# The first group of an adaLN transformer block: two projection tiles ahead of the rest, first attention slots loaded ahead of other stores, TensorE run on transposes before its work

## The chip, the core and the metric

One core of one Trainium2 chip runs the whole program. The metric is device microseconds of one execution; the median of three runs counts. Engines: PE is TensorE (matmuls and transposes, results in PSUM), DVE is VectorE, ACT is ScalarE, POOL is GpSimd, SP is SyncE, whose queue issues nearly all DMAs here. Each engine works through its own instructions in the order in which they were written; engines wait for each other by semaphores.

## The reference, cut to what matters

```python
x = A_x                                   # 1 x 2048 x 448, f32
mod = (silu(c) @ w_mod).reshape(1, 6, 1, -1)
sa, ca, ga, sb, cb, gb = (mod[:, 0], ..., mod[:, 5])
h = layernorm(x) * (1 + ca) + sa
# A: 16 heads of 28, causal window of 256
qkv = h @ wqkv
p = softmax(where(mask, q @ k.T * 28 ** -0.5, -1e9))
x = x + ga * ((p @ v) @ wo)
h = layernorm(x) * (1 + cb) + sb
x = x + gb * (mish(h @ w1 + b1) @ w2)     # 448 -> 1792 -> 448
```

## The kernel before

All products are kept near f32 precision by splitting each operand into a rounded part (names with `h` or hi) and the rest (`l`, lo) and adding three products. A 448-deep contraction is therefore 11 matmuls (`passes`, L183), taken over four chunks `ci` of 128 rows; the last chunk holds hi and lo of its 64 rows stacked.

The 2048 tokens are four groups `g` of 512 (`GT`). For each group the program normalises x (`gen_ln1`), transposes it (`tr`, four chunks of four 128x128 transposes) and applies the scale and shift columns `cols`, which gives `hh` and `hl` (`hT_hi` on ACT, `hT_y` and `hT_lo` on DVE). It then projects: tiles 0 to 6 are 128 rows of the q and k features each (q is features 0 to 447, k is 448 to 895, so tile 3 holds the end of q and the beginning of k), tiles v0 to v3 are V of 128 tokens each. `qk_out` (L308) takes a q/k tile out of PSUM (hi by ACT, lo by DVE) and stores it to the DRAM scratch `scr`: two DMAs for a tile of q rows or of k rows alone, four for tile 3, which has both.

Attention goes by slots: slot i is head i % 16 of group i // 16. `L(i)` (L562) loads q and k of a slot from `scr`. `A(i, t)` (L571) is a pass for the row maxima: a matmul `sA` on PE, then a max over it (`junk`, `mx`) on DVE. `M2` (L584) turns the maxima of two slots into rows (`mt` on PE, `mr` on DVE) and two small DMAs put them below q (`q<-mr`). `B(u)` (L600) is the score matmul proper (`sB`), exp on ACT (`P`, `Ph`), `SP` the rest `Pl` on POOL, `PV` the product with V. There are three units u per slot; the main loop (L920) runs B, SP, PV of its unit, the A of three slots ahead (`LEAD`), and between them takes steps of a filler, `fill_main(g)`, at `RATE[g]` credit per unit (about one microsecond of matmuls is one credit). The filler of group 0 holds what is left of group 0's projections, then the transposes and projections of group 1. `fill_side` carries the layernorm `ln1` of the next group and weight preparation, one step per unit from u = 2 on. At u = 48 the rest of group 0's fillers is drained; from there on before and after have the same instructions in the same order.

Ahead of the loop, in order: loads of c (`cT`), x of group 0, the first 896 columns of w_mod in four pieces `wm01`, then wqkv (`wqs`) in three parts of columns (`QCOLS`). DVE sums c-weighted pieces of w_mod into `acc01` (`mod_sum`, L143), PE turns that into columns (`mc`, L152), DVE copies them to `cols`. Splits of wqkv are shared by ACT (hi) and DVE and POOL (lo, `wql`). Three tiles, 0, 3 and 4, are worked through together (L397 to L401), stored, then `load_slot` loads slots 0 to 3, v0 to v3 and the tiles 1 and 5 run, and the A of slots 0 to 2 go with tiles 5, 2 and 6. `need` keeps running the filler until the tiles that a slot reads have been written.

Of the kernel before, what the change touches and what calls it, by code (L numbers as in the profile page):

```python
# [8 lines left out]
F32 = mybir.dt.float32  # L9
# [10 lines left out]
NEG = -1.0e30  # L20
# [31 lines left out]
def adaln_block(ctx: ExitStack, tc: tile.TileContext, x, wqkv, wo, w1, b1, w2, c, w_mod, out):  # L52
# [19 lines left out]
    vp, vp_s = pool("vp")  # L72
    st0, st0_s = pool("st0")
# [3 lines left out]

    ACT.add_instruction(mybir.InstLoadActFuncSet(
# [54 lines left out]
    cols = cst.tile([128, 4, 4], F32, name="cols")  # L133

# [3 lines left out]
    DVE.tensor_scalar(sT, sT, 1.0, None, op0=ALU.add)  # L138
    DVE.reciprocal(sT, sT)
    DVE.tensor_tensor(sT, sT, cT, op=ALU.mult)  # L140
# [100 lines left out]
    def hT_lo(p, ci, hh, hl, si):  # L241
        hT_y(p, ci, si)
        DVE.tensor_tensor(hl[:, ci], p, hh[:, ci].bitcast(F32), op=ALU.subtract)
# [58 lines left out]
    later = []  # L302

# [4 lines left out]
    def qk_out(g, m, p, st=None):  # L308
        st = st or qk.tile([128, 2, GT], F32R, name=f"st{g}_{m}", tag="qs", bufs=3)
# [11 lines left out]

        def put():
            for a, b, pa, ph in ((0, qn, 0, 2), (qn, 128, 1, 0)):
                if a < b:
                    dma(scr[r0 + a:r0 + b, pa:pa + 2, gs], st[a:b].bitcast(F32))
                    dma(scr[r0 + a:r0 + b, ph, gs], st[a:b, 0].bitcast(F32))
            done.add((g, m))

        return hi, lo, store

# [17 lines left out]
    def gen_qkv(g, tiles):  # L348
        first = {"v2": ("sB", 2), "v3": ("sB", 2), 1: ("pv", 1), 5: ("tr", 1)} if g == 0 else {}
        for m in tiles:  # L350
            p = bank(*first.get(m, ("mm", 2)), f"qk{g}_{m}")
# [17 lines left out]
    for k in range(4):  # L369
        mod_sum(k, wm01[k], acc01)  # L370
    pm = bank("sA", 2, "mc01")
# [8 lines left out]
    for ci in range(4):  # L380
        hi = wq3[:, ci, c0:c1]
        split_hi(wqs[ci][:, c0:c1], hi, ACT)
        split_lo(wqs[ci][:, c0:c1], hi, wql[:, min(ci, 2), c0:c1], ci, POOL)
    for i in range(2):
# [6 lines left out]
    for c0, c1 in QCOLS[1:]:  # L391
        for ci in range(4):
            split_hi(wqs[ci][:, c0:c1], wq3[:, ci, c0:c1], ACT)
    for (c0, c1), eng in zip(QCOLS[1:], (DVE, POOL)):
        for ci in range(4):
            split_lo(wqs[ci][:, c0:c1], wq3[:, ci, c0:c1], wql[:, min(ci, 2), c0:c1], ci, eng)
    first = [(m, bank(tag, b, f"qk0_{m}"), qk_passes(0, m)) for m, tag, b in ((0, "pv", 1), (3, "tr", 1), (4, "sA", 2))]  # L397
    for lo_n, hi_n in ((0, 3), (3, 6), (6, 11)):
        for m, p, ps in first:
            for n in range(lo_n, hi_n):  # L400
                PE.matmul(p, ps[n][1], ps[n][0], start=(n == 0), stop=(n == 10))  # L401
    for m, p, ps in first:
        st = st0.tile([128, 2, GT], F32R, name="st0_4") if m == 4 else None
        for f in qk_out(0, m, p, st):
            f()
        flush()
    st0_s.close()
    att, att_s = pool("att")

    identr = att.tile([128, 128], BF16, name="identr")  # L410
    mask = att.tile([128, 384], F32, name="mask")
# [656 lines left out]
```

## Time and profile before

| | |
|---|---|
| median of 3 runs | 740.03 us (738.38, 740.03, 742.38) |
| profiled execution | 743.38 us |
| its span, first to last instruction | 741.6 us |
| PE busy | 695.8 us, 94% |
| DVE, ACT, POOL busy | 378.9, 392.8, 331.4 us |
| moved by DMA | 83.86 MB |

How to read it: the page gives busy time by engine and the chain of work that ended last; the timeline lists instructions with their start, their length, and, in brackets, how long the engine had idled and what ended that; `x31` merges 31 like instructions that follow each other. PE's instructions overlap, so the price of one in a row of them is the distance between starts and not its length. [...] A matmul row is up to 0.4 us long though one can start each 0.23 us.

### The profile page before, as it was taken

The page shows a single profiled execution, that of the slowest core. Times are in us where ns is not written, and L with a number is a line of the kernel's source. Part 1 is how long each engine was busy: PE and PEld are TensorE (multiplying, and loading weights), DVE is VectorE, ACT ScalarE, POOL GpSimd, SP SyncE. Part 2 cuts the span into 40 slices and gives each one's busy share as a digit, 9 for nine tenths or more (in the row PEclk, how much of TensorE's full clock was granted, in tenths as well). Part 3 has the DMA queues.
Part 4 walks back from the last instruction along what each step waited for, and adds up shares of the span by engine and source line. Part 5 has one row for each costly group of instructions (what it writes and reads, how often), then busy time and mean ns, then how long its engine had stood idle before and what let it go on. Part 6 is the DMA issues. An engine that isn't in the chain of part 4 may idle for free.

```text
span 741.6 us, 11907 instructions
## 1 busy us (share of the span) xinstructions
PE 695.8 (94%) x3969; PEld 591.2 (80%) x3969; DVE 378.9 (51%) x1009; ACT 392.8 (53%) x740; POOL 331.4 (45%) x358
## 2 busy tenths in 40 slices
PE   3988989999999999999999889999999999999996
PEld 2866768778789888888887768878888888888885
DVE  4768546596765587665567843342323232413113
ACT  4416767676766677667778883343223222322221
POOL 4714788586666586666778854522010000000000
PEclk9898989999999999999999999999999999999999
DMA  8766644355274364453476155500200020001001
GB/s 211 204 226 221 166 139 129 94 178 179 86 226 154 100 221 144 133 179 92 145 215 204 50 187 164 145 24 1 100 0 1 1 99 1 1 0 50 1 0 50
DMA packets 48121, 83.86 MB, mean 113 GB/s; under 512 B 6126, under 2 KB 26108, under 8 KB 48060
## 3 DMA queue, kind: packets, MB, share of 16 engines
q1 hardware_dynamic: 48060, 83.10, 37.0%
q8 instruction: 32, 0.52, 0.3%
q14 instruction: 29, 0.24, 0.1%
HBM read 53.45 MB, written 29.36 MB: 112 GB/s over the span
## 4 chain that ended last, share of the span: by engine, by line
PE 77%; DVE 9%; DMA 7%; issue 3%; ACT 2%; POOL 1%; SPq 1%; DVEq 0%; POOLq 0%; ACTq 0%
PE z L813 19%; PE pv L639 9%; PE qk L294 6%; PE acc L990 6%; PE acc L991 6%; PE acc L989 6%; PE qk_v L294 5%; PE sA L578 4%; PE wo L294 4%; PE sB L608 4%; DMA k<-scr 3%; PE sB L619 3%; DVE junk L580 3%; PE et L650 1%; PE qk L401 1%
## 5 line engine op out<-in xcount | busy, mean ns | idle before, releaser
L629 POOL TENSOR_TENSOR Pl<-P,Ph 128x512 fp32r<-128x512 f32 (+2 forms) x192 | 236.7, 1240 | 94.0 <-ACT Ph L623 53.4
L580 DVE CUSTOM_DVE_ANT_0 junk<-sA,mask 128x384 f32<-128x384 f32 (+2 forms) x256 | 134.9, 527 | 116.7 <-PE sA L578 112.7
L622 ACT ACTIVATE P<-sB 128x512 f32<-128x512 f32 (+2 forms) x192 | 109.9, 572 | 65.0 <-PE sB L619 62.7
L821 DVE TENSOR_TENSOR al<-t,ah 128x512 fp32r<-128x512 f32 x56 | 38.8, 692 | 204.9 <-ACT ah L820 204.9
L819 ACT ACTIVATE t<-z,b1c 128x512 f32<-128x512 f32 x56 | 38.6, 689 | 193.3 <-PE z L813 182.4
L578 PE MATMUL sA<-k,q 84*128 84x384 f32 (+2 forms) x256 | 102.3, 403 | 10.7 <-DVE mx L580 6.0
L623 ACT ACTIVATE Ph<-sB 128x512 fp32r<-128x512 f32 (+2 forms) x192 | 109.3, 569 | 0.0
L813 PE MATMUL z<-hhf,w 128*128 128x512 f32 x224 | 89.4, 399 | 0.0
L813 PE MATMUL z<-hlf,w 128*128 128x512 f32 x224 | 88.7, 396 | 0.0
L989 PE MATMUL acc<-w2h,ah 128*128 128x448 f32 x224 | 82.2, 367 | 0.0
L990 PE MATMUL acc<-w2l,ah 128*128 128x448 f32 x224 | 82.0, 366 | 0.0
L991 PE MATMUL acc<-w2h,al 128*128 128x448 f32 x224 | 81.9, 366 | 0.0
L639 PE MATMUL pv<-Ph,v 128*60 128x256 f32 (+2 forms) x352 | 77.6, 294 | 3.0 <-ACT o L644 2.5
L639 PE MATMUL pv<-Pl,v 128*60 128x256 f32 (+2 forms) x352 | 74.5, 286 | 2.2 <-POOL Pl L629 2.1
L608 PE MATMUL sB<-q,k 86*128 86x256 f32 (+1 forms) x352 | 75.2, 288 | 1.0 <-DMA q<-mr 1.0
L813 PE MATMUL z<-hhf,w1l 128*128 128x512 f32 x168 | 66.4, 395 | 0.0
L608 PEld LDWEIGHTS sB<-q,k 86*128 86x128 f32 x352 | 62.6, 192 | 2.6 <-issue 1.0
L578 PEld LDWEIGHTS sA<-k,q 84*128 84x128 f32 x256 | 50.3, 197 | 16.8 <-DVE mx L580 10.1
L619 PE MATMUL sB<-fdmask,identr 128*128 128x128 bf16 (+1 forms) x320 | 60.9, 256 | 0.0
L639 PEld LDWEIGHTS pv<-Ph,v 128*60 128x60 f32 x352 | 45.5, 134 | 19.0 <-ACT o L644 6.0
L639 PEld LDWEIGHTS pv<-Pl,v 128*60 128x60 f32 x352 | 45.5, 133 | 11.8 <-POOL Pl L629 4.8
L644 ACT ACTIVATE o<-pv 60x512 f32<-60x512 f32 x64 | 37.8, 591 | 30.3 <-PE pv L639 29.8
(148 smaller groups left out, 1257.5 us busy)
## 6 DMA issues: line engine op xcount, KB each, us to landing
scr<-st SPq DMA_DIRECT2D x24, 512.0 KB
k<-scr SPq DMA_DIRECT2D x48, 252.0 KB
q<-scr SPq DMA_DIRECT2D x64, 168.0 KB
scr<-st SPq DMA_DIRECT2D x32, 256.0 KB
x<-x1d SPq DMA_DIRECT2D x10, 448.0 KB
xin<-in_A_x_dram SPq DMA_DIRECT2D x8, 448.0 KB
xr<-in_A_x_dram SPq DMA_DIRECT2D x16, 224.0 KB
x1d<-xr SPq DMA_DIRECT2D x16, 224.0 KB
```

The costliest lines, as they stand in the source:

```text
L294: PE.matmul(p, b, a, start=(n == 0), stop=(n == 10))
L578: PE.matmul(p[:, c0:384], q[0:84, t * 128:(t + 1) * 128], k[0:84, t * 128 + c0:t * 128 + 384], start=True, stop=True)
L580: DVE.tensor_tensor_reduce(out=junk[:, c0:384], in0=p[:, c0:384], in1=mask[:, c0:384], scale=1.0, scalar=-3.0e38, op0=ALU.add, op1=ALU.max ...
L608: PE.matmul(p[:, c:c + 128 * (t1 - t0)], k[:, jj * 128:(jj + 1) * 128], q[:, t0 * 128:t1 * 128], start=(n == 0), stop=False, skip_group_ch ...
L622: ACT.activation(P[:, c0:], p[:, c0:], AF.Exp, scale=SCALE)
L623: ACT.activation(Ph[u][:, c0:], p[:, c0:], AF.Exp, scale=SCALE)
L629: POOL.tensor_tensor(Pl[u][:, c0:], Pt[u][:, c0:], Ph[u][:, c0:].bitcast(F32), op=ALU.subtract)
L639: PE.matmul(pv[0:60, t0 * 128:t1 * 128], V[j % NV][:, h, :], P[u][:, c:c + 128 * (t1 - t0)], start=(P is Ph and b == 0 and n == 0), stop=F ...
L813: PE.matmul(zb[n], ps[m][1], ps[m][0], start=(m == 0), stop=(m == 10))
L989: PE.matmul(p, ah[n][:, ts], w2h[f], start=(f == 0), stop=False)
L990: PE.matmul(p, ah[n][:, ts], w2l[f], start=False, stop=False)
L991: PE.matmul(p, al[n][:, ts], w2h[f], start=False, stop=(f == NF - 1))
```

## The change

Only group 0 changes, up to unit 48:

- The load of c is issued from ACT's queue, ahead of everything; the fourth piece of w_mod is loaded and summed in two halves of 448 columns. The three small DVE steps on c come after the statistics of x.
- 64 transposes of the identity (`warm`) are added on PE: 50 ahead of the transposes of x, 2 after each of the first three token tiles, 8 behind `mc`.
- Constants (mask, the -1 rows of five k buffers, `fdf`) are made earlier on POOL, in a new pool `kq`.
- Two of the four `hT_y` steps go from DVE to ACT; splits of wqkv are spread in another order.
- Tiles 0 and 3 alone are worked through first. The k half of tile 3 and tile 0 are stored, then slots 0 and 1 are loaded, then come the other half of tile 3, tile 4, slots 2 and 3, and only then x of group 1.
- v0, v1 and tile 1 precede the first maxima; after that every A is followed by a filler step of up to four matmuls. Tile 6, the statistics of group 1's layernorm and all its transposes now stand in the main loop; side steps of group 0 start at u = 0; `RATE[0]` is 0.53.

```diff
+    cT = cst.tile([112, 4], F32, name="cT")
+    nc.scalar.dma_start(cT, c.rearrange("o (k p) -> p (o k)", p=112))
...
-    cT = cst.tile([112, 4], F32, name="cT")
-    dma(cT, c.rearrange("o (k p) -> p (o k)", p=112))
     x_load(0)
     wm01 = []
     for k in range(4):
         t = st0.tile([112, 2 * D], F32, name=f"wm01_{k}")
-        dma(t, w_mod[k * 112:(k + 1) * 112, 0:2 * D])
+        for s in (slice(0, 2 * D),) if k < 3 else (slice(0, D), slice(D, 2 * D)):
+            dma(t[:, s], w_mod[k * 112:(k + 1) * 112, s])
...
+        parts = [lambda: rows(qn, 128, 1, 0), lambda: rows(0, qn, 0, 2)]
+
         def put():
-            for a, b, pa, ph in ((0, qn, 0, 2), (qn, 128, 1, 0)):
...
+            while parts:
+                parts.pop(0)()
             done.add((g, m))
...
+    wb = bank("tr", 1, "warm")
+    def warm(n):
+        for _ in range(n):
+            PE.transpose(wb[:, 0:128], ident, ident)
+    warm(50)
...
+        if t < 3:
+            warm(2)
     for i in range(2):
         mod_cols(acc01[:, i * D:(i + 1) * D], pm[:, 4 * i:4 * i + 4])
+    warm(8)
...
     for ci in range(4):
         hT_hi(trs[ci], ci, hh, 0)
-        hT_lo(trs[ci], ci, hh, hl, 0)
-    x_load(1)
...
+        if ci % 2:
+            first_split(2 + ci // 2)
+            ACT.activation(trs[ci], trs[ci], AF.Identity, scale=cols[:, 1, ci:ci + 1], bias=cols[:, 0, ci:ci + 1])
+        hT_lo(trs[ci], ci, hh, hl, 0, ci % 2 == 0)
...
+    first_tiles([(0, bank("pv", 1, "qk0_0")), (3, bank("tr", 1, "qk0_3"))])
+    for m in (0, 3):
+        PARTS[0, m].pop(0)()
+    PARTS[0, 0].pop(0)()
+    L(0)
+    L(1)
+    flush()
+    split_cols(*QCOLS[1], (None, None, POOL, POOL))
+    first_tiles([(4, bank("sA", 2, "qk0_4"))])
+    flush()
...
-            yield from gen_qkv(0, VT + (1, 5, 2, 6))
+            yield from gen_qkv(0, VT[:2] + (1,) + VT[2:] + (5, 2, 6))
...
-    RATE = {0: 0.48, 1: 0.88, 2: 0.88, 3: 0.62}
+    RATE = {0: 0.53, 1: 0.88, 2: 0.88, 3: 0.62}
...
-    for i in range(LEAD + 1):
+    for i in range(2, LEAD + 1):
         load_slot(i)
-    need({f"v{t}" for t in range(4)}, 0)
-    load_slot(LEAD + 1)
+    x_load(1)
+    for _ in range(9):
+        fill0()
...
     for i in range(LEAD):
         for t in range(4):
             A(i, t)
-            if t % 2:
-                pipe.step()
-                next(fillers[0])
-                flush()
-            side_step(0)
+            fill0()
         if i % 2:
-            pipe.step()
-            next(fillers[0])
             M2(i // 2)
+            load_slot(LEAD + 1)
...
-            if v > 1:
+            if v > 1 or g == 0:
                 side_step(g)
```

On SP's queue, the first stores to `scr` (tiles as `st_` and the tile's number) and the first loads of q and k, before:

```order
L59 DMA scr<-st_0_291 128x2x512
L59 DMA scr<-st_0_291 128x512
L59 DMA scr<-st_3_296 64x2x512
L59 DMA scr<-st_3_296 64x512
...
L59 DMA scr<-st_4_303 128x2x512
L59 DMA scr<-st_4_303 128x512
L59 DMA q_0_350<-scr 84x512
L59 DMA k_0_353<-scr 84x512
```

and after:

```order
L59 DMA scr<-st_3_384 64x2x512
L59 DMA scr<-st_3_384 64x512
L59 DMA scr<-st_0_381 128x2x512
L59 DMA scr<-st_0_381 128x512
L59 DMA q_0_352<-scr 84x512
L59 DMA k_0_136<-scr 84x512
...
L59 DMA k_1_138<-scr 84x512
...
L59 DMA scr<-st_4_413 128x2x512
```

Eight stores stood ahead of the first load, now four do.

On PE, where the first transposes of group 1 (`tr`) stand, before, in the unit of the first score matmul:

```order
L294 MATMUL qk_6_541<-hl_223,wq_96 128x512
L578 MATMUL sA_2_577<-k_2_357,q_1_351 128x384
L578 MATMUL sA_3_581<-k_2_357,q_1_351 128x384
L232 MATMUL tr_587<-ident,xin_236 128x128 x4
L608 MATMUL sB_597<-q_0_350,k_0_353 128x384
```

and after, in unit 4:

```order
L661 MATMUL sB_708<-q_0_352,k_1_138 128x256
L672 LDWEIGHTS identr
L672 MATMUL sB_708<-fdmask,identr 128x128
L631 MATMUL sA_1_717<-k_4_144,q_2_433 128x256
L309 MATMUL qk_6_625<-hl_307,wq_100 128x512
L246 MATMUL tr_738<-ident,xin_456 128x128 x4
```

Tile 6 and the transposes have moved behind the first score matmuls, the transposes right behind the last matmul of tile 6.

On DVE, the end of group 1's statistics and the four normalising steps (`xin<-xin,mva,rsa`), which these transposes read, before:

```order
L193 BN_AGGR mva_483<-sta_513 128x2
L580 ISA junk,mx_479<-sA_0_519,mask 128x128
...
L222 TENSOR_SCALAR xin_236<-xin_236,mva_483,rsa_516 128x448
L580 ISA junk,mx_479<-sA_2_532,mask 128x384
...
L580 ISA junk,mx_479<-sA_3_537,mask 128x384
...
L317 TENSOR_TENSOR st_2_528<-qk_2_491,st_2_528 128x512
L588 CAST mr_555<-mt_553 8x128
```

and after:

```order
L207 BN_AGGR mva_630<-sta_700 128x2
L633 ISA junk,mx_687<-sA_1_717,mask 128x256
L633 ISA mx_687 128x1
L236 TENSOR_SCALAR xin_456<-xin_456,mva_630,rsa_703 128x448
L333 TENSOR_TENSOR st_6_725<-qk_6_625,st_6_725 128x512
L236 TENSOR_SCALAR xin_456<-xin_456,mva_630,rsa_703 128x448 x3
```

The normalising steps were spread between maxima; now one stands ahead of the lo step of tile 6 and three behind it, in one run.

## Rows read from the trace of the kernel before

**Rows 1.** The page: span of the profiled execution.
```profile
span 741.6 us, 11907 instructions
```
**Rows 2.** Windows of three stages: busy us of each engine, granted clock, DMA.
```profile
18.10:56.40 38.30, 34.49 (x139) 26.65 (x139) 27.91 (x63) 13.24 (x23) 17.29 (x45) 0.91 0.70 214
56.40:73.30 16.90, 14.74 (x83) 12.01 (x84) 13.62 (x35) 11.03 (x24) 8.09 (x8) 0.80 0.68 219
73.30:140.00 66.70, 60.54 (x388) 48.65 (x387) 37.31 (x143) 47.75 (x111) 51.31 (x54) 0.95 0.50 139
```
**Rows 3.** Chain that ended last, in order of time: start, us, what.
```profile
38.52 5.12 PE qk L294 x22
```
**Rows 4.** Windows of 1 us: granted clock is the third number from the end.
```profile
17.00:18.00 1.00, 0.00 (x0) 0.00 (x0) 0.40 (x4) 1.00 (x3) 0.92 (x2) 1.00 1.03 373
18.00:19.00 1.00, 0.87 (x2) 0.50 (x2) 0.85 (x2) 1.00 (x3) 0.43 (x1) 0.51 0.88 247
25.00:26.00 1.00, 1.00 (x6) 0.82 (x5) 1.00 (x2) 0.54 (x1) 1.00 (x2) 1.00 0.98 364
```
**Rows 5.** Timeline of SP, the first issues.
```profile
0.73 0.39 SPq L59 DMA_DIRECT2D cT<-in_c_dram  x1
1.18 0.98 SPq L59 DMA_DIRECT2D xin<-in_A_x_dram  x2
```
**Rows 6.** Timeline of DVE: last sum of w_mod, first scale step, last hl, lo steps.
```profile
13.40 1.15 DVE L147 SCALAR_TENSOR_TENSOR acc<-wm,sT,acc 112x896 f32<-112x896 f32 x1 [0.31 <-DMA wm<-in_w_mod_dram]
18.11 0.82 DVE L236 TENSOR_SCALAR tr<-tr,cols 128x512 f32<-128x512 f32 x1 [0.69 <-ACT hh L239]
23.32 0.69 DVE L243 TENSOR_TENSOR hl<-tr,hh 128x512 fp32r<-128x512 f32 x1
29.56 1.89 DVE L317 TENSOR_TENSOR st<-qk,st 128x512 fp32r<-128x512 f32 x3
```
**Rows 7.** Timeline of ACT: the four hh steps.
```profile
17.30 2.79 ACT L239 ACTIVATE hh<-tr,cols 128x512 fp32r<-128x512 f32 x4
```
**Rows 8.** Timeline of SP: first stores, first loads, a store and the load behind it.
```profile
30.27 6.91 SPq L59 DMA_DIRECT2D scr<-st  x8
37.29 1.19 SPq L59 DMA_DIRECT2D q<-scr  x1
...
42.59 0.90 SPq L59 DMA_DIRECT2D scr<-st  x2
48.75 0.32 SPq L59 DMA_DIRECT2D q<-scr  x1
```
**Rows 9.** Timeline of PE: first maxima, first mt, first score matmul, that of unit 48.
```profile
43.48 0.40 PE L578 MATMUL sA<-k,q 84*128 84x128 f32 x2
...
52.38 0.27 PE L586 MATMUL mt<-ident,mx 128*8 128x128 f32 x1 [0.38 <-DMA scr<-st]
...
56.37 0.41 PE L608 MATMUL sB<-q,k 86*128 86x384 f32 x1 [0.61 <-DMA q<-mr]
...
139.85 0.47 PE L608 MATMUL sB<-q,k 86*128 86x384 f32 x2
```
**Rows 10.** Timeline of POOL: the power step of group 1's layernorm.
```profile
49.35 1.05 POOL L207 TENSOR_TENSOR rsa<-rsa,mhalf 128x4 f32<-128x4 f32 x1
```
**Rows 11.** Timeline of DVE: the first normalising step of group 1.
```profile
50.44 0.51 DVE L222 TENSOR_SCALAR xin<-xin,mva,rsa 128x448 f32<-128x448 f32 x1 [0.80 <-POOL rsa L207]
```
**Rows 12.** PE's waits from 56.4 to 140 us: total, times, longest.
```profile
PE sA L578 <- DMA k<-scr: 3.7, 2, 2.8
PE tr L232 <- DVE hl L243: 2.2, 2, 1.1
```
**Rows 13.** Timeline of SP ahead of the longest of them.
```profile
89.54 3.01 SPq L59 DMA_DIRECT2D scr<-st  x4
...
93.48 0.51 SPq L59 DMA_DIRECT2D k<-scr  x1
```
**Rows 14.** Timeline of PE behind that load.
```profile
97.54 0.44 PE L578 MATMUL sA<-k,q 84*128 84x128 f32 x1 [2.85 <-DMA k<-scr]
```

More of the change, by code (lines that the diff above doesn't have):

```diff
@@ L133, in adaln_block, with k3_tile @@
     cols = cst.tile([128, 4, 4], F32, name="cols")
+    K3 = []
+    def k3_tile(pl, i):
+        t = pl.tile([86, GT + W], F32R, name=f"k3_{i}")
+        POOL.memset(t[64:86, :].bitcast(F32), -1.0)
+        K3.append(t)
+    for i in range(NK - 1):
+        k3_tile(kq, i)
+    mask = kq.tile([128, 384], F32, name="mask")
+    POOL.memset(mask, 0.0)
+    POOL.affine_select(mask, mask, pattern=[[1, 384]], compare_op=ALU.is_ge, fill=NEG, base=-1,
+                       channel_multiplier=-1)
+    POOL.affine_select(mask, mask, pattern=[[-1, 384]], compare_op=ALU.is_ge, fill=NEG, base=W,
+                       channel_multiplier=1)
     sT = cst.tile([112, 4], F32, name="sT")
     ACT.activation(sT, cT, AF.Exp, scale=-1.0)
-    DVE.tensor_scalar(sT, sT, 1.0, None, op0=ALU.add)
-    DVE.reciprocal(sT, sT)
-    DVE.tensor_tensor(sT, sT, cT, op=ALU.mult)
     def mod_sum(k, w, acc):
@@ L302, in adaln_block @@
     later = []
+    PARTS = {}
     def flush():
@@ L348, in gen_qkv @@
     def gen_qkv(g, tiles):
-        first = {"v2": ("sB", 2), "v3": ("sB", 2), 1: ("pv", 1), 5: ("tr", 1)} if g == 0 else {}
         for m in tiles:
-            p = bank(*first.get(m, ("mm", 2)), f"qk{g}_{m}")
+            p = bank("mm", 2, f"qk{g}_{m}")
             if isinstance(m, str):
@@ L368, in adaln_block @@
         next(ln0)
-    for k in range(4):
+    DVE.tensor_scalar(sT, sT, 1.0, None, op0=ALU.add)
+    DVE.reciprocal(sT, sT)
+    DVE.tensor_tensor(sT, sT, cT, op=ALU.mult)
+    for k in range(3):
         mod_sum(k, wm01[k], acc01)
+    for s in (slice(0, D), slice(D, 2 * D)):
+        mod_sum(3, wm01[3][:, s], acc01[:, s])
+    wb = bank("tr", 1, "warm")
[3 more added lines that the diff above has]
+    warm(50)
     pm = bank("sA", 2, "mc01")
@@ L376, in adaln_block, with first_split @@
             PE.transpose(trs[ci][:, t * 128:(t + 1) * 128], XS[0][t][:, ci * 128:(ci + 1) * 128], ident)
+        if t < 3:
+            warm(2)
     for i in range(2):
         mod_cols(acc01[:, i * D:(i + 1) * D], pm[:, 4 * i:4 * i + 4])
+    warm(8)
     c0, c1 = QCOLS[0]
-    for ci in range(4):
+    def first_split(ci):
         hi = wq3[:, ci, c0:c1]
@@ L388, in adaln_block @@
         hT_hi(trs[ci], ci, hh, 0)
-        hT_lo(trs[ci], ci, hh, hl, 0)
-    x_load(1)
[L391 to L405, printed above, removed]
-        flush()
[L407 to L411, printed above, removed]
-    POOL.memset(mask, 0.0)
-    POOL.affine_select(mask, mask, pattern=[[1, 384]], compare_op=ALU.is_ge, fill=NEG, base=-1,
-                       channel_multiplier=-1)
-    POOL.affine_select(mask, mask, pattern=[[-1, 384]], compare_op=ALU.is_ge, fill=NEG, base=W,
-                       channel_multiplier=1)
-    fdf = att.tile([128, 512], F32, name="fdf", tag="P", bufs=3)
+        if ci % 2:
+            first_split(2 + ci // 2)
+            ACT.activation(trs[ci], trs[ci], AF.Identity, scale=cols[:, 1, ci:ci + 1], bias=cols[:, 0, ci:ci + 1])
+        hT_lo(trs[ci], ci, hh, hl, 0, ci % 2 == 0)
+    for v in V:
+        POOL.memset(v[:, :, 28:29].bitcast(F32), 1.0)
+        POOL.memset(v[:, :, 29:32].bitcast(F32), 0.0)
+    fdf = kq.tile([128, 256], F32, name="fdf")
     POOL.memset(fdf[:, 0:256], 0.0)
@@ L898, in load_slot, with fill0 @@
         L(i)
-    for i in range(LEAD + 1):
+    def fill0():
+        pipe.step()
+        next(fillers[0])
+        flush()
+    for i in range(2, LEAD + 1):
         load_slot(i)
-    need({f"v{t}" for t in range(4)}, 0)
-    load_slot(LEAD + 1)
+    x_load(1)
+    for _ in range(9):
+        fill0()
     DVE.tensor_copy(identr, ident)
-    DVE.tensor_copy(fdmask, fdf[:, 0:256])
+    DVE.tensor_copy(fdmask, fdf)
     for i in range(LEAD):
@@ L971, in adaln_block @@
             PV(u - 2, Ph)
-    for st in (FW["s2"], att_s, vp_s):
+    for st in (FW["s2"], att_s, kq_s, vp_s):
         st.close()
```

70 lines of the change are left out of this document (45 added, 25 removed).

## Prediction, made before the result was known

> **What bounds the kernel now.** The span is 741.6 us [rows 1] and its execution took 743.38. From unit 48 of the main loop on, near 140 us, the change leaves every instruction where it was, so only the first 140 us count. I read that part in the order of the windows by stage, the timeline of PE in each, and then SP's timeline wherever PE waited for a transfer. From 18.1 us PE is the engine with the most work in every stage [rows 2]: it is busy for 34.5 of 38.3 us up to the first score matmul, 14.7 of 16.9 in the units with group 1's transposes, 60.5 of 66.7 after that. At full clock 22 matmuls of 512 columns take 5.12 us, 0.233 each [rows 3]; I take 0.233 x 448 / 512 = 0.204 for those of V. The stages lose time in three ways. Nothing runs on the projections until the column sums are there; ACT's first hh step starts at 17.30 [rows 7]. Then the granted clock falls to 0.5 at 18 us, behind a microsecond in which PE did nothing, and is back at 25 [rows 4]. Third, PE waits for loads of k, 3.7 us in two waits [rows 12], and the mean clock of 0.95 in that stage [rows 2] means 0.05 / 0.5 x 66.7 = 6.7 us more at half.
>
> The work before unit 48 is fixed, about the same matmuls before and after. So the change is worth what it takes from three sums: the start, PE's waits, and the time at half clock.
>
> **The start.** Without c's load in front, SP's first x load issues at 0.73 instead of 1.18: 0.45 us [rows 5], if transfers all move with it. The last sum over w_mod takes 1.15 us behind the arrival of its piece [rows 6]; of two halves only the second, some 0.58, is left behind it. Together the columns, and the first hh, come 1.0 us sooner, at 16.3. The lower end is nothing (POOL now makes five k buffers and the mask ahead of group 0's statistics); the upper is 2, if transposes and `mc` run at full clock as well. The 64 added transposes lie in time in which PE waits for x and for the columns; if their cover were gone the 50 would push x's transposes back.
>
> **The first two tiles.** Before, from the first hh to the end of the last hl it is 6.7 us (17.30 to 23.32 + 0.69) [rows 6, 7]. ACT now takes two of the four scale steps of 0.82 [rows 6], but its own list grows by them and by two splits; I take 5.8 us, so hl is done at 22.1. At full clock PE has then some six matmuls left, 1.5 us: both tiles are out at 23.6. A hi step on ACT and a lo step on DVE later, 1.89 / 3 = 0.63 for the lo [rows 6] and as much for the hi, with the hand-overs near 25.1, the first store can go; before it went at 30.27 [rows 8]. That is 5.2 us sooner.
>
> **The first loads.** Four stores, 1.15 MB, now stand ahead of slot 0's load. Before, from the first store to the load's issue it was 7.0 us with eight stores, and for tile 1's 0.77 MB 6.2 us from store to the load that waits for it [rows 8]. I take 6, so the loads issue at 31.1; k of a slot arrived 4.1 us behind its issue in a busy stretch [rows 13, 14], and I take 3.4 with a queue that has run empty. The first maxima matmul is then at 34.5, before 43.48 [rows 9]: 9.0 us sooner. PE itself would be ready at 23.6 + 11 x 0.233 (tile 4) + 22 x 0.204 (v0, v1) + 2.56 (tile 1) = 33.3, and so waits 1.2 us.
>
> [...]
>
> **From the first maxima to the first score matmul.** PE has v2 and v3 (4.5), tiles 5 and 2 (5.1) and twelve maxima matmuls of some 0.2: 12 us, to 46.5. The other way round, `mt` comes at 42.5 and from `mt` to the first score matmul it was 4.0 us before (52.38 to 56.37) [rows 9], again 46.5. But the two small loads of the maxima now stand on SP behind tile 4's and tile 1's stores, slots 2 and 3 and 0.9 MB of x; I add 0.9 us: 47.4, before 56.37. The gain up to here is **9.0 us**.
>
> **What is given back.** (a) Tile 6 was done by then and now is not: 11 x 0.233 = 2.56 us, and one chunk of transposes, 0.45: **3.0 us** of PE work moved behind. (b) The transposes of group 1 now follow tile 6's last matmul directly, and they read all four normalised tiles. Those wait for POOL's power step (1.05 us [rows 10], and a short step ahead of it, 1.35 in all behind the last statistics) and then for DVE: one normalising step of 0.45 (0.51 long [rows 11], the next begins before its end), tile 6's lo step of 0.63, which itself waits for tile 6, and three more normalising steps, 1.3. That is 3.7 us from the last statistics, which DVE ends when PE ends tile 6. PE stands still for about that long, and the maxima, scores and P x V of unit 5 queued behind the transposes stand with it; DVE's and POOL's lists also wait for them. Before, this was spread among maxima, and PE waited there for hl, 2.2 us in two waits [rows 12], of which I expect 1.8 again. Net **3.3 us**. It costs 1.5 if DVE runs ahead of PE here, 5 if a `Pl` subtraction holds up the power step on POOL. (c) Every normalising and statistics step that used to lie between maxima now adds to DVE's list in the first units; that is in (b).
>
> **What else moves.** The longest wait, 2.85 us for k [rows 14], came behind four stores of tile 3 of group 1, 3.01 us of issuing [rows 13], and two loads of wo ahead of these. With group 1's projections some ten units later, those wo loads no longer stand between the maxima's rows and the stores; half of that wait should go, **1.3 us**. The bounds are 0 and, with the wait wholly gone and the half-clock stretch behind it too (6.7 us, so up to 3.4), 6.3. `RATE` only spreads the same matmuls; 0.53 x 48 = 25.4 credits cover the 24 of work left.
>
> **Sum.** -9.0 + 3.0 + 3.3 - 1.3 = **-4.0 us**, 743.38 to 739.4 for the profiled execution. That execution is 3.35 above the median of the three runs; on the median it is 740.03 - 4.0 = **736.0 us**. About 0.5%, 3.7 us, is what a measurement of this kernel can tell from no change, so the forecast lies on the edge of it.
>
> **Rivals.** First, *the clock is not held*. In the trace the clock is full from 17 to 18 us, behind the transposes of x and `mc`, and falls as PE waits for the first hh [rows 4]. The first 50 of the added transposes will be over by then; behind them come again `mc`, eight transposes, a wait for hh and one for the first hl. If it falls there, the 22 matmuls cost twice their 5.1 us, of which some 2.4 pass while PE would wait for hl anyway: they end 2.7 us later and all loads with them, 738.7. For it: the same thin stretch is still there. Against: two of its waits are filled. [...]
>
> Second, *more of the k waits goes*, with the half-clock stretch behind them: another 3.4 us, 732.6. For it: that stretch follows the one wait. Against: the stores of tile 3 still stand ahead of the next slots.
>
> Third, *slower*: SP's single queue. Slots 2 and 3 wait for tile 4's store to land; if that takes 6.2 us and more behind the loads of slots 0 and 1, they come near 45, x and tile 1's store then hold the maxima's rows back to 51, and the first score matmul is 4.5 us later than forecast; slots 4 to 6 then come late too, a wait of 3.7 us as in [rows 12], all in all -4.0 + 8.2 = +4.2: 744.2. It decides from a queue that moves under about 200 GB/s between 31 and 51 us; the stage had 214 [rows 2].
>
> Fourth, the change *does not do what it says*: PE waits for the loads just as long as it was busy before, and only the start is won, less what (b) costs: 740.
>
> **Chances.** Forecast 0.42 (734.2 to 737.8), clock not held 0.22, more waits gone 0.18, slower 0.11, nothing done 0.07. Faster by over 0.5% are the second rival, 0.25 of the forecast's 0.42 and 0.02 of the first: 0.45. Slower is the third, 0.11. The rest, 0.44, is within. The range reaches from the second rival's 732.6 less a run's scatter (731) to between the fourth and the third: 742.5.
>
> **What would show it.** After: first `hh` near 16.3; granted clock 1.00 from 17 to 25; first store issue near 25; first `sA` near 34.5 with a wait for `k<-scr` of about 1 us; first `sB` near 47.4; then one wait of PE of 3 to 4 us ahead of `tr<-ident,xin`, released by DVE; unit 48's first `sB` near 136 instead of 139.85 [rows 9]. Wrong would be a clock of 0.5 in the first tiles, waits for `k<-scr` or `q<-mr` over 2 us before 60, or a time that differs behind unit 48.

## The result, and the profile after

The changed kernel is slower: ratio to the kernel before 1.0041, 95% interval 1.0022 to 1.0060, over 21 runs of each (medians 745.74 and 742.38 us). That is 3.0 us more, where 4.0 less was forecast. The profiled execution took 748.40 us. Its page, and the same stages as [rows 2] (stage bounds moved with the first score matmul and the transposes; columns as there):

```profile
span 746.6 us, 12035 instructions
```
```profile
18.20:53.90 35.70, 30.38 (x132) 24.48 (x131) 20.58 (x53) 14.56 (x26) 11.11 (x32) 0.93 0.61 184
53.90:71.40 17.50, 13.69 (x57) 10.43 (x57) 11.04 (x33) 7.26 (x16) 7.36 (x12) 0.71 0.65 209
71.40:140.10 68.70, 63.94 (x428) 51.77 (x427) 43.97 (x158) 52.61 (x120) 54.25 (x56) 1.00 0.53 153
```

PE's timeline, the rows that answer to [rows 3, 9], with the transposes of group 1 and the first score matmul of unit 48:

```profile
1.34 7.89 PE L404 MATMUL warm<-ident 128*128 128x128 f32 x50 [1.34 <-POOL ident masks.py:199]
11.47 0.66 PE L412 MATMUL tr<-ident,xin 128*128 128x128 f32 x4 [2.24 <-ACT xin L232]
...
15.04 3.25 PE L166 MATMUL mc<-ones,acc 112*128 112x1 f32 x16
...
19.83 0.77 PE L471 MATMUL qk<-hh,wq 128*128 128x512 f32 x1
...
38.27 0.30 PE L631 MATMUL sA<-k,q 84*128 84x128 f32 x1 [0.30 <-DMA k<-scr]
...
45.92 0.27 PE L639 MATMUL mt<-ident,mx 128*8 128x128 f32 x1
...
53.98 0.66 PE L661 MATMUL sB<-q,k 86*128 86x384 f32 x1 [3.48 <-DMA q<-mr]
...
65.77 0.33 PE L246 MATMUL tr<-ident,xin 128*128 128x128 f32 x1 [2.89 <-DVE xin L236]
...
140.10 0.47 PE L661 MATMUL sB<-q,k 86*128 86x384 f32 x2
...
445.30 0.63 PE L246 MATMUL ot<-ident,on 128*128 128x128 f32 x4 [2.20 <-ACT w L178]
```

Read it from the top. The 50 transposes end at 9.2, PE stands 2.24 us until ACT hands over x, and behind that pause the clock goes to half, as the windows say (granted clock, as a share of full speed, is the third number from the end, as in [rows 4]):

```profile
11.50:12.70 1.20, 1.20 (x11) 1.18 (x12) 1.17 (x3) 1.20 (x3) 0.45 (x2) 1.00 1.00 283
12.80:15.00 2.20, 2.20 (x12) 2.20 (x11) 0.07 (x1) 1.40 (x3) 1.58 (x4) 0.50 0.37 87
...
23.00:27.00 4.00, 4.00 (x19) 3.23 (x18) 2.95 (x6) 2.46 (x5) 3.07 (x24) 1.00 0.00 0
```

The first maxima come 5.2 us sooner than in [rows 9], `mt` 6.5 sooner, but the first score matmul only 2.4: from `mt` to `sB` it is now 8.1 us, before it was 4.0. SP's queue says why (start, duration of issuing, what; this answers to [rows 8]):

```profile
28.41 2.71 SPq L59 DMA_DIRECT2D scr<-st  x4
34.63 0.38 SPq L59 DMA_DIRECT2D q<-scr  x1
...
44.96 0.91 SPq L59 DMA_DIRECT2D xin<-in_A_x_dram  x2
45.92 0.97 SPq L59 DMA_DIRECT2D scr<-st  x2
46.99 1.80 SPq L59 DMA_DIRECT2D q<-mr  x2
```

The maxima's rows (`q<-mr`) go out behind x of group 1 and a tile's store, and PE waits 3.48 us for them. Then it stands 2.89 us ahead of the transposes of group 1. In return the long waits for k and the half clock of [rows 12, 14] are nearly gone: the clock is 1.00 from 71.4 to 140.1. So unit 48 starts at 140.10, before 139.85. The time at half clock ahead of it has not shrunk, it has moved: the stretches that began at 18.0, 59.0 and 96.5 us now begin at 12.7, 53.7 and 67.4, 20.5 us in all in both kernels. The whole of what stands ahead of unit 48, before and after:

```profile
0.00:139.85 139.85, 115.53 (x639) 92.09 (x639) 87.18 (x261) 78.98 (x167) 85.48 (x124) 0.93 0.61 178
```
```profile
0.00:140.10 140.10, 122.62 (x702) 100.99 (x703) 83.21 (x260) 79.47 (x169) 83.78 (x124) 0.93 0.60 178
```

The other 4.8 us of this execution's loss come behind unit 48, where both kernels have the same instructions in the same order: 606.5 us from unit 48 to the end, before 601.8. A part of it is at 445.30: PE stands 2.20 us ahead of the first `ot` transposes (attention's output of the last group, at the change to the feed-forward stage). Before, PE went straight on there and waited 0.92 a little later:

```profile
440.45 0.60 PE L232 MATMUL ot<-ident,on 128*128 128x128 f32 x4
...
444.85 0.63 PE L232 MATMUL ot<-ident,on 128*128 128x128 f32 x4 [0.92 <-DVE hlo L511]
```

### The profile page after: what moved, and what is told of

Read it like the earlier page. It is cut to its first block, busy times and chain, and to the rows that moved or that the text cites. A ratio compares the mean times of both kernels' runs of the same rounds, so it can differ in the third digit from the quotient of the medians.

```text
span 746.6 us, 12035 instructions
## 1 busy us (share of the span) xinstructions
PE 703.8 (94%) x4033; PEld 600.3 (80%) x4033; DVE 375.0 (50%) x1008; ACT 393.0 (53%) x742; POOL 329.3 (44%) x358
## 4 chain that ended last, share of the span: by engine, by line
PE 74%; DVE 8%; DMA 6%; ACT 3%; issue 2%; POOL 1%; SPq 1%; DVEq 0%; POOLq 0%; ACTq 0%
PE z L866 19%; PE pv L692 8%; PE qk L309 7%; PE acc L1044 6%; PE acc L1045 6%; PE acc L1043 6%; PE sA L631 5%; PE qk_v L309 4%; PE sB L661 4%; DMA k<-scr 4%; PE wo L309 4%; PE sB L672 3%; DVE junk L633 2%; DMA q<-mr 1%; PE et L703 1%
```

## Experiments

Each row is one kernel: ratio of its runs to those of the kernel before, the start of unit 48 in its trace, and the time from there to the end. Times are in us; a difference of 0.001 in the ratio is 0.74 us, and two ratios nearer to each other than about 0.003 are not apart by their intervals.

| kernel | ratio (95%) | unit 48 at | behind it |
|---|---|---|---|
| before, two traces | 1 | 139.85, 140.22 | 601.8, 601.5 |
| changed, two traces | 1.0041 (1.0022 to 1.0060) | 140.10, 139.30 | 606.5, 602.7 |
| no_warm | 1.0025 (1.0001 to 1.0049) | 141.25 | 601.2 |
| warm_gap | 0.9999 (0.9981 to 1.0017) | 136.84 | 602.0 |
| x_late | 0.9978 (0.9960 to 0.9996) | 133.63 | 604.6 |
| ct_sp | 1.0010 (0.9992 to 1.0028) | 138.89 | 602.0 |
| x_early | 0.9959 (0.9926 to 0.9992) | 135.41 | 601.2 |
| x_early_warm | 0.9925 (0.9884 to 0.9965) | 127.11 | 603.2 |
| late_stats | 0.9906 (0.9877 to 0.9935) | 132.08 | 603.0 |
| tr_first | 1.0055 (1.0030 to 1.0080) | 140.79 | 601.8 |
| bank_fix | 1.0030 (1.0012 to 1.0048) | 141.76 | 601.8 |
| bank_pv | 1.0005 (0.9984 to 1.0026) | 140.79 | 600.7 |
| nm_dve | 1.0026 (1.0002 to 1.0050) | 135.37 | 606.0 |
| best | 0.9917 (0.9893 to 0.9940) | 136.00 | 600.2 |
| best2 | 0.9918 (0.9889 to 0.9946) | 134.05 | 600.7 |
| best3 | 0.9865 (0.9835 to 0.9895) | 127.23 | 601.5 |

### The clock at the start: no_warm, warm_gap

```diff
-    warm(50)          # no_warm: and warm(2), warm(8)
+    warm(72)          # warm_gap
...
-    warm(8)
+    warm(20)          # warm_gap
```

> Without any of the 64 added transposes. Theory A (the warm-up buys nothing, since PE stands 2.24 us behind it and the clock is at half from 12.7 on): the transposes of x now begin at half clock near 11.4, the column sums run at full, the clock is at half again under the first tiles until about 25, both tiles are out near 27 as with the warm-up (26.9), first sA near 38.3, and the time is that of the changed kernel within 1 us. Rival (the warm-up itself pulls the clock down early, since its full stretch ends before the tiles, and without it the fall comes later and lasts shorter): the tiles are out near 25 and the time falls by 2 us. Second rival (it does help, the half stretch ends at 23 because of it): the tiles are out at 29 and the time rises by 2 us.

Without the transposes the first maxima came at 40.84 (changed: 38.27 and 37.70) and unit 48 at 141.25, some 1.5 us later than the 139.7 of the changed kernel's two traces; yet the time is not higher. It has 601.2 us behind unit 48. So in the traces the warm-up did win a little ahead, against theory A and less than the second rival's 2, and something that came with it lost as much behind.

> 72 transposes instead of 50 ahead of those of x, and 20 instead of 8 behind the column sums, so that the idle 2.24 us and the wait for the first hh are filled. Theory A (the clock fell because PE stood still ahead of x): full clock from 5.9 to 23 and beyond, column sums in 2.0 us instead of 3.25, first hh near 17.4 instead of 18.97, tiles out near 25.0 instead of 26.9, first sA near 36.4, unit 48 1 to 2 us sooner, the time 1 to 2 us less. Rival (16 column sums of one column do not count as work and the clock falls anyway): half from about 16 to 23, tiles out at 26 to 27, time unchanged within 1 us.

PE's timeline of warm_gap:

```profile
11.41 0.66 PE L412 MATMUL tr<-ident,xin 128*128 128x128 f32 x4 [0.18 <-ACT xin L232]
...
13.87 1.90 PE L166 MATMUL mc<-ones,acc 112*128 112x1 f32 x16
...
17.86 0.48 PE L471 MATMUL qk<-hh,wq 128*128 128x512 f32 x1
```

With the pause filled (0.18 us left) the column sums took 1.90 instead of 3.25, the first projections came 2.0 us sooner, and the granted clock fell for the first time at 49.5, in the wait for `q<-mr`. A part of that is scatter. In a second trace of the changed kernel (after_again, below) PE stood only 1.50 us ahead of x, the column sums ran at full clock without any edit, and the clock fell at 17.6, right behind PE's wait for the first hh:

```profile
11.45 0.69 PE L412 MATMUL tr<-ident,xin 128*128 128x128 f32 x4 [1.50 <-ACT xin L232]
...
14.00 1.90 PE L166 MATMUL mc<-ones,acc 112*128 112x1 f32 x16
...
17.42 0.63 PE L471 MATMUL qk<-hh,wq 128*128 128x512 f32 x1 [0.49 <-ACT hh L253]
```
```profile
17.70:24.40 6.70, 6.17 (x15) 4.29 (x15) 5.17 (x8) 4.76 (x9) 4.06 (x25) 0.50 0.63 189
```

Against that trace warm_gap's first projections are no sooner, but its first maxima come 2.5 us sooner (35.21 for 37.70), and so does unit 48. The column sums did not cost the clock: it stayed full through them here. The edit fills two places, the pause ahead of x and the wait for the first hh. That the first is the one that counts is shown by nm_dve (below): it keeps the eight transposes behind the column sums, its pause ahead of x is 0.49 us, and its clock stays full to 51.6. So theory A is right on cause. Unit 48 came some 3 us sooner than in the changed kernel's two traces and the time fell by about as much (1.0041 to 0.9999).

### SP's queue: x_late, x_early, late_stats

x_late issues x of group 1 behind the maxima's rows. x_early issues it where it stood before the change, and spreads group 1's statistics over the maxima again; x_early_warm adds the 72 and 20 transposes; late_stats is x_early_warm with the statistics left where the change put them.

```diff
-    x_load(1)                       # ahead of the first maxima
...
             M2(i // 2)
+            x_load(1)               # x_late
```
```diff
         hT_lo(trs[ci], ci, hh, hl, 0, ci % 2 == 0)
+    x_load(1)                       # x_early
...
             A(i, t)
             fill0()
+            side_step(0)            # x_early
...
-            if v > 1 or g == 0:
+            if v > 1:               # x_early
```

> The load of x of group 1 is issued behind the maxima's rows of slots 0 and 1 instead of ahead of tile 1's store. Theory B (single SP queue: 0.9 MB of x and 0.77 MB of tile 1 stand ahead of those rows): the wait of PE for q<-mr falls from 3.48 to under 1.5 us, the first sB comes near 51.5 instead of 53.98; unit 48 2 to 3 us sooner, and if the half clock from 53.7 to 60.5 was caused by that wait and goes too, 5 to 6 us; the time falls by that. Rival (given back): x lands later by as much, the statistics of group 1 and its four normalising steps come later, PE's wait ahead of the transposes of group 1 (2.89 us) grows by 2 to 3 us, unit 48 and the time stay within 1 us.

First score matmul at 48.87 instead of 53.98, unit 48 at 133.63. PE's timeline:

```profile
48.87 0.33 PE L661 MATMUL sB<-q,k 86*128 86x384 f32 x1
...
58.92 0.43 PE L246 MATMUL tr<-ident,xin 128*128 128x128 f32 x1 [3.28 <-DVE xin L236]
```

No wait for the maxima's rows is left; PE's stand ahead of group 1's transposes grew by 0.4, not by 2 to 3. Theory B holds: from the issue of the rows to the first score matmul it was 7.0 us with x in front of them (46.99 to 53.98) and is 3.7 without (45.14 to 48.87), so x cost 3.3 us there. Of the 5.1 us by which the first score matmul is sooner, 1.4 came ahead of `mt`, where the edit changes nothing on PE (here a half-clock stretch of 3.4 us at the start, there one of 10.2). The time fell by 4.7 us (1.0041 to 0.9978); by the two intervals it can be 2.7 to 6.6.

> x of group 1 is loaded where it was before the change, behind the first hl, into the time in which the DMA engines move next to nothing (32 and 4 GB/s from 22 to 26 us), and the statistics of group 1 take a step with every maxima matmul, as before. Theory B (SP's one queue and the late statistics are what the change gives back): first stores and first sA at the same time within 1 us, wait for q<-mr under 1.5 us, first sB near 49 to 51, PE's wait ahead of the transposes of group 1 (3.3 us with x behind the rows) under 1 us; unit 48 at 129 to 132 instead of 140.1; the time 5 to 8 us under the changed kernel's. Rival (DVE's list is full in 38 to 55: statistics between the maxima hold mx and mt back): first sB at 53 and later, unit 48 no sooner than 134. A second one, for behind unit 48: time won ahead of it is in part lost behind it, in all kernels; then 604 us or more from unit 48 to the end and a time only 3 to 5 us less.

Theory B held only in part. PE's wait for the normalising steps is gone, as two of its waits from 50 to 70 us show (total, times, longest; a third, of 1.2, is that of the projections for hl):

```profile
PE tr L246 <- DVE st L333: 1.6, 1, 1.6
PE tr L246 <- DVE hl L258: 1.3, 1, 1.3
```

But in this trace the clock was at half from 12.4 to 15.8, behind a pause of 2.75 us ahead of x, and again from 19.2 to 26.0, so the first maxima came at 39.38 and unit 48 at 135.41. From the first maxima to `mt` it was 9.1 us instead of 7.65: the statistics between the maxima do hold DVE up (x_early_warm and late_stats, which differ in that alone, have 9.1 and 7.6), and in that the rival is right. The time is some 6 us under the changed kernel's (0.9959 against 1.0041).

> The same with 72 and 20 transposes, which fill PE's idle time ahead of x and of the first hh. If the two gains add up: unit 48 3 us sooner than with x early alone, 126 to 129, the time another 2 to 3 us less, 7 to 10 under the changed kernel's and 5 to 7 under the kernel before. If the rule is that what is won ahead of unit 48 is partly lost behind, half of that. If the full clock at the start is given back by a half-clock stretch soon after: unit 48 within 1 us of x early.

With the pause filled the gains added up: first maxima at 35.43, first score matmul at 48.53, unit 48 at 127.11, and no half-clock stretch in the whole trace up to 726 (mean granted clock 0.997).

> x early with 72 and 20 transposes, but the statistics and normalising steps of group 1 at the place that the change gave them, from the first unit of the main loop on. Theory (the bunched steps make PE stand ahead of the transposes of group 1, whenever x lands): first maxima rows mt at 42.8 instead of 44.5, first sB near 47, then 3 to 3.6 us of waiting for the normalising step, unit 48 2 us later than with the statistics among the maxima, 129. Rival (the stand is worth no more than what the statistics cost among the maxima): unit 48 within 0.7 us of 127.1. Second rival: a half-clock stretch behind that wait, unit 48 near 131.

Here `mt` came at 43.37 and `sB` at 47.84, PE stood 3.3 us for the normalising step, the clock was at half from 58.5 to 65.3, and unit 48 came at 132.08: the second rival, in the trace. The times of this kernel and x_early_warm are not apart (0.9906 on four runs, 0.9925 on seven), so what the bunched steps cost is shown as a place, not as a time.

### Behind unit 48: a bank of PSUM

> The changed kernel, a second trace, for the stretch behind unit 48, where it has the same instructions in the same order as before and took 606.5 us in its first trace, against 601.8 before, 601.2 without the added transposes, 602.0 with c on SP's queue and with more transposes, 604.6 with x late. If the 4.8 us are scatter of runs (half-clock stretches and waits for k that come and go): 601 to 605 here, and unit 48 at 139 to 142. If they belong to the change: 605.5 or more.

> The kernel before, a second trace: unit 48 near 139.9 if the stretch ahead of it repeats within 1 us; behind it 600 to 604 if that part scatters, 601.8 within 0.5 if it doesn't, which would leave the change as the cause of what comes behind unit 48.

The changed kernel's second trace had 602.7 us there, the first had 606.5; before repeated within 0.3. So up to 3.8 of the 4.8 us were scatter, but not all: in all ten traces in which the first tile of PSUM is of tag `tr` PE stands 2.20 us ahead of the first `ot`, and in none of the other eight. (A tag names the tiles of a pool that take turns in the same bank or banks.) The instruction lists show a wait there that the kernel before does not have:

```
after    ot <- ident,on  128x128   [waits DVE, ACT]
before   ot <- ident,on  128x128   (acc, three instructions later, waits for DVE, ACT)
```

The transposes go to `bank("tr", 1, "warm")`, now the first PSUM tag in use. The banks of the feed-forward stage come from the pool that takes over; which old bank a new tile inherits depends on the order in which the tags were first used. In the second trace of the changed kernel `ot` starts at 441.94, 0.15 us behind DVE's last read of the last `et` (attention's output of a pair of slots, of tag `tr`):

```profile
441.45 0.34 DVE L717 TENSOR_TENSOR ol<-ol,et 128x224 f32<-128x224 f32 x1
```

The programs as built give the bank numbers: this `ot` is in bank 0 in every one of them. The tag first in use gets bank 0 too. In the kernel before that is `sA`, and the last `et` is in bank 7, as in all kernels without the wait; in the changed kernel it is `tr`, and the last `et` is in bank 0, as in all kernels with the wait. So `ot` has inherited the bank of this `et`. That the order makes the wait is shown by the next runs.

```diff
+    wb = bank("tr", 1, "first")                     # tr_first: the kernel BEFORE
+    PE.transpose(wb[:, 0:128], ident, ident)
     pm = bank("sA", 2, "mc01")
```
```diff
-    wb = bank("tr", 1, "warm")
+    pm = bank("sA", 2, "mc01")                      # bank_fix: transposes into pm
```
```diff
-    wb = bank("tr", 1, "warm")
+    pm = bank("sA", 2, "mc01")                      # bank_pv
+    trs = [bank(("sB", "mm")[ci // 2], 2, f"tr0{ci}") for ci in range(4)]
+    wb = bank("pv", 1, "warm")
```

> The kernel before with one more transpose of the identity, ahead of everything on PE, into a bank of tag tr, which so is the first tag in use. Theory C (bank order): unit 48 within 0.6 us of 140, a wait of 2.2 us at the first ot transpose near 440 us and none of 0.9 at the later one, 603 to 604 us from unit 48 to the end, the time 1.3 to 2.9 us more than the kernel before. Rival (the wait is a matter of timing and not of the bank): 601.5 to 602 behind unit 48 and no difference in time.

One transpose, 0.2 us of work in idle time, made the kernel before 0.55% slower, about 4.1 us (2.2 to 5.9), more than the 1.3 to 2.9 expected. PE's timeline of its trace has the wait:

```profile
441.98 0.63 PE L232 MATMUL ot<-ident,on 128*128 128x128 f32 x4 [2.20 <-ACT w L164]
```

That trace, the fastest of its eleven executions, lost only 2.4 at this place, won 1.1 back at the next `ot`, and had 601.8 us behind unit 48, not the 603 to 604 expected. The wait itself is thus 1.3 us; where the rest of the 4.1 comes from is not shown (the order moves the banks of the other tags too). The clock is one candidate. In five of the ten traces with the wait a half-clock stretch of 3.4 us begins between 434 and 447 us, in none of the eight without, and behind unit 48 those five have 604.4 us on average, the other five 602.2, the eight 601.2. The mean granted clock of the runs does not settle it: it is 0.9825 against 0.9874 of the kernel before, which is 2 x 0.0049 x 745 = 7 us more at half, but bank_pv (below), without the wait, has no more than 0.9838 against 0.9865.

> The changed kernel with one edit: the 64 transposes write into the bank of the column sums (tag sA) and no longer into one of tag tr, so that the PSUM tags of the attention stage are first used in the order that they had before. Theory C (the order in which tags are first used sets which bank the first ot transpose inherits at the change of stages near 440 us; with tr first it is the bank that the last et step still reads, and PE stands 2.20 us there in every trace with the added transposes, and not in those of the kernel before or without them, which wait 0.9 to 1.0 us at the ot chunk behind it): no wait at the first ot, 0.9 to 1.0 at the later one; from unit 48 to the end 601 to 602 us (602.0 to 606.5 with the wait); unit 48 at 139 to 140.5; the time 1.3 us less than the changed kernel's, and up to 2.9 less where a half-clock stretch followed the wait. Rival (the wait is only the first of two that PE would meet anyway): the time behind unit 48 stays at 602.7 and more.

The wait at the first `ot` was gone and 1.42 came at the later one, 601.8 us behind unit 48, but the time stayed (1.0030). The edit had a price of its own: DVE's copy of the columns now waited for the eight transposes behind the column sums, since both are in one bank. PE, then DVE, of bank_fix:

```profile
16.68 1.90 PE L166 MATMUL mc<-ones,acc 112*128 112x1 f32 x16
18.51 1.09 PE L404 MATMUL mc<-ident 128*128 128x128 f32 x8
```
```profile
19.64 0.16 DVE L171 TENSOR_SCALAR cols<-mc 128x3 f32<-128x3 f32 x1 [6.91 <-PE mc L404]
```

> The changed kernel, the banks of the column sums and of the transposes of x first, and the 64 added transposes into one of tag pv, which no engine but PE touches until the first tile: the tags are in use in the order of the kernel before. Theory C: no wait at the first ot transpose, 601 to 602 us behind unit 48, unit 48 at 139 to 140.5, first hh as in the changed kernel (16.6 or 19.0, by the clock), the time 2 to 4 us less than the changed kernel's, so within 1 us of the kernel before or 1 us under it. Rival (the order costs nothing here, since what it costs in the kernel before hangs on the time at which PE comes to it): the ratio to the kernel before stays at 1.003 to 1.004.

With the order put back and the columns free, the ratio went from 1.0041 to 1.0005, some 2.7 us (0.6 to 4.8 by the two intervals), and 600.7 us remain behind unit 48. Over all traces that stretch is 603.3 us on average with tag `tr` first (ten) and 601.2 without (eight).

### The start of x: ct_sp, nm_dve

```diff
-    nc.scalar.dma_start(cT, c.rearrange("o (k p) -> p (o k)", p=112))
+    dma(cT, c.rearrange("o (k p) -> p (o k)", p=112))          # ct_sp
```
```diff
-            POOL.tensor_tensor(nm, mv[:, :, 0], rs, op=ALU.mult)
-            POOL.tensor_scalar(nm, nm, -1.0, None, op0=ALU.mult)
+            DVE.scalar_tensor_tensor(nm, mv[:, :, 0], -1.0, rs, op0=ALU.mult, op1=ALU.mult)   # nm_dve
```

> The load of c goes back to SP's queue, ahead of x, as before the change. Theory (c on ACT's queue moves beside x and slows it; first statistics of x at 4.82 instead of 4.48): first statistics at 4.5, first hh 0.3 us sooner, unit 48 within 0.5 us, time unchanged within 1 us. Rival for what is lost behind unit 48 (606.5 us from unit 48 to the end in the profile, 601.8 before, with the same instructions): a second DMA queue in use is what slows it; then this kernel has 602 us behind unit 48 and its time falls by 3 us.

The first transposes of x began at 10.58 instead of 11.47, more than the landing of x explains (first statistics 4.64 instead of 4.82). Both signs of the rival came, 602.0 us behind unit 48 and a time 2.3 us less (1.0041 to 1.0010), where the theory had none. It falls by other runs all the same: no_warm, bank_pv and best3 have c on ACT's queue and 601.2, 600.7 and 601.5 us there, and here the wait of 2.20 at `ot` stays. What differs at the start is a small step on POOL. In the changed kernel, DVE and POOL:

```profile
9.07 1.15 DVE L161 SCALAR_TENSOR_TENSOR acc<-wm,sT,acc 112x896 f32<-112x896 f32 x1
```
```profile
9.37 0.91 POOL L225 TENSOR_TENSOR nma<-mva,rsa 128x4 f32<-128x4 f32 x1
```

The POOL step takes 0.20 in the kernel before and here 0.91: it began inside DVE's sum over w_mod and ended 0.06 us behind it. With c and w_mod loaded sooner, the sum starts sooner, just there. What makes the step wait is not shown.

> The changed kernel with the two small steps on the statistics of x (nma) as one on DVE, between the first and the second sum over w_mod, instead of two on POOL. Theory D (a small POOL step that begins beside one of these sums, 1.15 us, ends only with it: 0.91 us instead of 0.20): ACT's first normalising step at 9.8 instead of 10.65, first transposes at 10.6 instead of 11.47, PE idle for 1.4 us ahead of them instead of 2.24, column sums finished at the same time or 0.5 sooner; first hh near 16.0 to 16.6; the time 0.5 to 2 us less. Rival (ACT waits for x or its own queue and not for nma): first transposes at 11.4 as before, no difference.

ACT's first step came at 9.52, the first transposes at 10.34, the column sums at full clock, the first hh at 15.98, as theory D has it. DVE, then PE and the granted clock:

```profile
9.32 0.16 DVE L225 SCALAR_TENSOR_TENSOR nma<-mva,rsa 128x4 f32<-128x4 f32 x1 [0.29 <-POOL rsa L221]
9.43 2.34 DVE L161 SCALAR_TENSOR_TENSOR acc<-wm,sT,acc 112x896 f32<-112x896 f32 x2
```
```profile
10.34 0.72 PE L413 MATMUL tr<-ident,xin 128*128 128x128 f32 x4 [0.49 <-ACT xin L231]
```
```profile
7.30:51.50 44.20, 36.82 (x200) 30.44 (x199) 26.28 (x67) 18.82 (x34) 15.99 (x40) 1.00 0.72 211
```

Unit 48 came at 135.37, 4.3 us sooner than in the changed kernel's two traces, but this trace has 606.0 us behind it. The time fell by about 1 us (1.0026), within the intervals of both, so that what the step is worth in time is not shown.

### All together: best, best2, best3

best is x_early_warm with the edit of bank_fix, best2 adds that of nm_dve with 66 transposes, best3 is best2 with the edit of bank_pv instead.

> x early, 72 and 20 transposes, and these in the bank of the column sums. If the gains add up: unit 48 near 127, 601.5 us from there to the end, the profiled span 728.5 to 730, the time 1 to 2 us under that of x early with more transposes, 734, and 8 to 10 us under the kernel before. If the wait at ot was covered by something else: no difference to x early with more transposes.

> The best version (x early, more transposes, these in the bank of the column sums) with the same edit and 66 transposes, since x is ready sooner. If D holds and the clock so stays full from 6 us on: first transposes at 10.6, first hh near 15.8, first sB near 47.5, unit 48 at 126 to 128, behind it 601 to 602, the time 733 to 735, 8 to 10 us under the kernel before. If the start is bound elsewhere: 736 as without it.

Neither was faster than x_early_warm: the transposes behind the column sums held the columns back here too (first hh at 19.95 and 18.85 us instead of 16.73).

> x early, nma on DVE, 66 and 20 transposes, these in a bank of tag pv. If the gains add up: first transposes at 10.4, first hh near 16, first sB near 47.5, unit 48 at 125 to 127, behind it 601 to 602, the time 731 to 733, 10 to 12 us under the kernel before (ratio 0.985). If bank and nma give nothing beside x and the clock: 735.5 to 737, as without them.

best3 beats both kernels: median 732.42 us against 743.45 of runs beside it; by the ratio 10 us. Its stages up to unit 48, to be laid beside [rows 2]:

```profile
18.00:48.00 30.00, 28.09 (x124) 21.95 (x124) 22.55 (x58) 12.12 (x23) 13.31 (x38) 1.00 0.76 234
48.00:66.00 18.00, 13.95 (x96) 11.01 (x95) 14.60 (x42) 12.99 (x28) 9.39 (x9) 1.00 0.79 249
66.00:127.00 61.00, 58.21 (x390) 47.75 (x388) 34.84 (x138) 47.13 (x109) 49.41 (x53) 1.00 0.53 157
```

The clock is 1.00 in all three. Unit 48 comes 12.6 us sooner than in [rows 9].

## Why the prediction was wrong, step by step

Between the 4.0 us less that were forecast and the 3.0 more that came lie 7: some 4 of them ahead of unit 48, 3 behind it. All three signs that the prediction named as wrong came: a clock of 0.5 in the first tiles, over 2 us of waiting for `q<-mr` (3.48), and a time that differs behind unit 48. (The 736.0 was also counted from a median of three runs, 740.03, that lies 2.4 under the median of 21.)

- **What counts (only the first 140 us).** Wrong, 3 us: the instructions behind unit 48 are the same, but one of their waits is not. The 64 transposes were costed as work in idle time, and that was right; the bank they write to was not costed at all. It is worth 2.1 us on average in the traces, 2.7 in time by bank_pv, and 4.1 alone in the kernel before.
- **The first hh, 16.3, a gain of 1.0.** It came at 18.97 and 16.59 in the two traces, before 17.30 [rows 7]. The sum over w_mod was ready 1.7 us sooner, even more than the 0.45 and 0.58 of [rows 5, 6]; but `mc` stands behind the transposes of x on PE, and these came 0.8 us later, mostly for the held POOL step. With `mc` at full clock (1.90, the second trace) the term is right to 0.3 us; at half (3.25, the first) it is a loss. The bound "nothing" was there, a loss was not.
- **The first tiles at full clock, 23.6.** They ended near 27 in the first trace and at 26 in the second. The first rival, the clock not held, was the case (a price of 2.7 in the prediction; warm_gap puts it at 2.5 to 3 us). In the second trace it fell where that rival said, at 17.6, behind the wait for the first hh; in the first it fell sooner, at 12.7, behind the pause ahead of x, which the prediction took for covered time. The 20.5 us at half clock ahead of unit 48, one of the prediction's three sums, were not reduced at all; best3 has none there.
- **Store to load, load to maxima.** 6.2 and 3.6 us where 6 and 3.4 were taken: right. PE's own 33.3 there adds up to 33.2, which changes nothing. The first maxima were 3.8 us late, 3.3 of it already at the first store.
- **From the first maxima to the first score matmul.** To `mt` 7.65 us (8 forecast); from there 8.1, where 4.0 and 0.9 were taken. This is the third rival's mechanism, x and tile 1's store ahead of the maxima's rows, 3.2 us here; the 0.9 was mis-sized. The sign by which that rival was to be known, a queue under about 200 GB/s between 31 and 51 us, did not come (232 and 244 in the two traces): the rows were late by their place in the queue, as x_late shows, where x behind them won about 4.7 us of time.
- **What is given back.** The stand ahead of group 1's transposes was 2.89 and 0.69 us, released by DVE, where about 3.7 was forecast: right, with its cause, as x_early shows.
- **Waits for k.** One of 1.74 us was left, and the half clock from 96.5 to 103.4 was gone: the second rival, worth more than the 1.3 us taken, by what was won back (below); no run has it alone.

Ahead of unit 48 the first score matmul came 6.6 and 6.1 us later than the 47.4 of the forecast, and 2.5 and 2.8 were won back behind it: unit 48 at 140.10 and 139.30, where 136 was forecast and 139.85 and 140.22 were measured before. That gains and losses come out even there is chance. Behind unit 48 the bank made a loss of it: with the old order of banks the ratio is 1.0005, neither faster nor slower (bank_pv). That a part of that loss comes by way of the clock is argued from where the half-clock stretches begin; no run set the clock alone.

## What to carry to other kernels

Where a change adds even one tile to a pool, compare the waits of the two programs to the end and not only the order of their instructions: who inherits which bank can change far behind the edit (here transposes from 1.34 us on brought a wait of 2.20 us near 440). Look at the pauses of PE ahead of its first real work when it is warmed up, and fill them to the end: with a pause left the warm-up won 1.5 us ahead of unit 48 here, with the pauses filled some 3 more. On a single DMA queue, a large load that nobody needs yet belongs into the time in which the DMA engines move nothing (0 GB/s from 23 to 27 us in the changed kernel), not ahead of a few small rows that PE will wait for (7.0 us from their issue to the first score matmul with x in front of them, 3.7 in x_late without).

## What was not expected of the hardware

- A pause of PE of 2.24 us, behind 7.9 us of transposes, was followed by 10 us at half clock (0.50 granted in the changed kernel, 12.7 to 23.0); with the pause at 1.50 us (after_again) the clock fell at 17.6; with 0.49 (nm_dve) and 0.18 (warm_gap) it stayed full (1.00) to 51.6 and 49.5.
- A 128 x 4 step on POOL that began inside a sum of 1.15 us on DVE took 0.91 and 0.90 us (the two traces of the changed kernel) and 1.13 (x_late) instead of 0.20 to 0.25; in no_warm, where it began 0.05 us behind the sum's start, it took 0.20.
- Profiled times behind unit 48 scatter by 3.8 us between executions of one program (606.5 and 602.7), with half-clock stretches and waits for k that come and go: a single trace can't price a stretch to better than that.
